# Start of a two-layer transformer kernel: the second x tile's statistics moved to ScalarE, the first rstd to GpSimd, and x tiles 2 and 3 loaded one Wq quarter later each

## Chip, cores and metric

The kernel runs on one core of one Trainium2 chip. The metric is the device time of one execution in microseconds. The profile's "span" is the part of an execution that the trace covers. It is somewhat shorter than the timed execution.

## The reference, cut to what matters

```
x = x + attention(layernorm(x))     # wqkv 1024 x 3072, sliding dilated window, wo
x = x + ffn(layernorm(x))           # 1024 -> 3584 -> 1024, gelu
# the same two lines once more (second layer, same weights)

def _layernorm(x, axis=-1, eps=1e-5):
    m = mean(x); v = var(x)
    return (x - m) / sqrt(v + eps)
```

The input x is 2048 x 1024 in bf16, which the kernel holds as 16 tiles of 128 rows. Nothing can be multiplied before the first tiles are loaded, normalised and transposed. The change is about that start alone.

## The kernel before

The first group of work is x tiles 0 to 3 and the weight Wq in four quarters of 512 KB, here called A to D. All are loaded by SP, in this order:

```
load_x(0, 0, 2)                        # x tiles 0 and 1
for k in range(0, KD, 2):
    load_wq_piece(wq_first[...], k)    # one quarter of Wq
    if k < 4:
        load_x(0, 2 + k // 2, 3 + k // 2)
# order: x0 x1 A x2 B x3 C D
```

The normalisation of the four tiles, in program order on VectorE (`vec`, DVE in the profile) and on ScalarE (`act`):

```
def stats(tt):
    ... two bn_stats and one bn_aggr on vec -> mvs[tt]
    act.activation(stds[tt][:], mvs[tt][:, 1:2], ACT.Sqrt, bias=eps_t[:])

def norm(tt, bounds=(0, D)):
    vec.reciprocal(rstd[:], stds[tt][:])
    ... vec.tensor_scalar: (x - mean) * rstd -> xn

stats(0); stats(1)
xn0 = norm(0); xn1 = norm(1, (0, 2 * P, D))
... 16 transposes of xn0 and xn1 on TensorE
stats(2); stats(3)
for tt in range(2, 4):
    first_late.append((norm(tt), ...))   # transposed later, among the matmuls
```

TensorE (PE) first runs 14 warm-up matmuls on zeros, then the transposes of tiles 0 and 1, then 36 half-width matmuls with quarters A to C, the transposes of tile 2, 16 more matmuls, the transposes of tile 3, and from there one unbroken run of 540 matmuls.

Of the kernel before, what the change touches and what calls it, by code (L numbers as in the profile page):

```python
# [8 lines left out]
ACT = mybir.ActivationFunctionType  # L9
ALU = mybir.AluOpType  # L10
AX = mybir.AxisListType
BF16 = mybir.dt.bfloat16
F32 = mybir.dt.float32
# [4 lines left out]
def kernel(  # L18
# [18 lines left out]
    P = 128  # L37
    _, S, D = A_x.shape
# [31 lines left out]
    lnp = ctx.enter_context(tc.tile_pool(name="lnp", bufs=2))  # L70
# [32 lines left out]
    vec, act, pool, sp = InOrder(nc.vector), InOrder(nc.scalar), InOrder(nc.gpsimd), InOrder(nc.sync)  # L103
# [15 lines left out]
    x = [xpool.tile([P, D], BF16, name=f"x{t}") for t in range(S // P)]  # L119

    def load_x(g, t0=0, t1=NTT):
        for tt in range(t0, t1):
            t = g * NTT + tt
            sp.dma_start(x[t][:], x_in[t * P:(t + 1) * P, :])
# [9 lines left out]
    def load_wq_piece(wt, k):  # L134
        sp.dma_start(wt[:, k % (KD // 2):k % (KD // 2) + 2, :], wqkv_v[:, k:k + 2, 0:D])
# [2 lines left out]
    wq_first = [wpool.tile([P, KD // 2, D], BF16, name="wt") for _ in range(2)]  # L138
    for k in range(0, KD, 2):
        load_wq_piece(wq_first[k // (KD // 2)], k)  # L140
        if k < 4:
            load_x(0, 2 + k // 2, 3 + k // 2)

    warm = bigp.tile([P, P], BF16, name="big")
    vec.memset(warm[:], 0.0)
    mhalf = const.tile([P, 1], F32, name="mhalf")
    pool.memset(mhalf[:], -0.5)
    eps_t = const.tile([P, 1], F32, name="eps_t")
# [59 lines left out]
    def transpose_on_pe(xn, out, parts):  # L208
        pst = psum.tile([P, KD, P], BF16, name="acc", bufs=8)
        for k in range(parts[0][0], parts[-1][1]):  # L210
            pe(nc.tensor.transpose(pst[:, k, :], xn[:, k * P:(k + 1) * P], ident[:]))  # L211
        for k0, k1, copy in parts:
            copy(out[:, k0:k1, :], pst[:, k0:k1, :])
# [10 lines left out]
    def ln_first():  # L224

        xa[0] = new_xnT()
        vec.on = act.on = True
        mvs = {}
        stds = {}

        def stats(tt):
            st6 = lnp.tile([P, 2, 6], F32, name="stats")
            for h in range(2):
                vec.bn_stats(st6[:, h, :], x[tt][:, h * HALF:(h + 1) * HALF])
            mvs[tt] = lnp.tile([P, 2], F32, name="mv")
            vec.bn_aggr(mvs[tt][:], st6[:])
            stds[tt] = lnp.tile([P, 1], F32, name="std")
            act.activation(stds[tt][:], mvs[tt][:, 1:2], ACT.Sqrt, bias=eps_t[:])

        def norm(tt, bounds=(0, D)):  # L240
            rstd = lnp.tile([P, 1], F32, name="rstd")
            vec.reciprocal(rstd[:], stds[tt][:])
            xn = lnp.tile([P, D], BF16, name="xn", bufs=3)
            for lo, hi in zip(bounds[:-1], bounds[1:]):
                vec.tensor_scalar(out=xn[:, lo:hi], in0=x[tt][:, lo:hi], scalar1=mvs[tt][:, 0:1], scalar2=rstd[:],
                                  op0=ALU.subtract, op1=ALU.mult)
            return xn

        stats(0)
        stats(1)  # L250
        xn0 = norm(0)
        xn1 = norm(1, (0, 2 * P, D))
        transpose_on_pe(xn0, xa[0][:, 0, :, :], [(0, 2, act.copy), (2, 8, act.copy)])
        transpose_on_pe(xn1, xa[0][:, 1, :, :], [(0, 2, vec.tensor_copy)])
        transpose_on_pe(xn1, xa[0][:, 1, :, :], [(2, 8, act.copy)])
        stats(2)
        stats(3)
        for tt in range(2, 4):
            first_late.append((norm(tt), xa[0][:, tt, :, :]))
        vec.on = act.on = False  # L260
        act.hold()

    def new_xnT(pool=None):
        return (pool or xnp).tile([P, NTT, KD, P], BF16, name="xnT")
# [350 lines left out]
    pool.on = True  # L615
    warm_up(14)
    ln_first()
    first = build_constants()
    with tc.tile_pool(name="early", bufs=1) as early:
# [62 lines left out]
```

## Time and profile before

| | before |
|---|---|
| time, median of 6 runs | 1230.29 us (1230.14 to 1230.75) |
| span of the profile | 1228.4 us |
| PE busy | 1221.6 us |
| 36 matmuls start, by the chain (8.26 by the timeline) | 8.40 us |
| weight loads of tile 2's transposes begin | 12.14 us |
| run of 540 matmuls starts | 14.89 us |

The prediction shows the chain and the timeline. Two views more are needed. First, PE's timeline, whose columns are start, length, engine, line, operation, output<-inputs, shape, count and, in brackets, the idle time before with its releaser:

```profile
0.99 6.02 PE L117 MATMUL acc<-big 128*128 128x512 bf16 x14 [0.99 <-DVE big L92]
7.05 1.35 PE L211 MATMUL acc<-ident,xn 128*128 128x128 bf16 x16
```

The warm-up matmuls were over at 7.01 us in this run, and the transposes came at once. Second, the list of DMA issues for two short stretches, one with x tile 3 (issued at 3.11 us) and one with quarter C (issued at 3.62 us). The last column is the time from issue to landing in us:

```profile
x<-in_A_x_dram SPq DMA_DIRECT2D x1, 256.0 KB, 6.8
wt<-in_A_wqkv_dram SPq DMA_DIRECT2D x1, 512.0 KB, 7.6
```

The tile landed at 9.9 us, the quarter at 11.2. The first x tile, with nothing in front of it, took 2.7 us. So a transfer issued at 3 us seems to spend most of its time behind the bytes in front of it.

### The profile page before, as it was taken

Reading aid. Unit: us, or ns where it says so; the run is one execution under the profiler, and the core shown is the slowest. Engines: PE = TensorE matmul, PEld = TensorE weight load, DVE = VectorE, ACT = ScalarE, POOL = GpSimd, SP = SyncE. Lnnn points to the kernel's source line nnn. Section 1 sums busy time; section 2 is a strip of 40 time slices with the busy share of each in tenths; the row PEclk is TensorE's granted clock in tenths of the full one; section 3 lists DMA queues with packets and bytes.
Section 4 is the critical chain, followed back from the end, with each engine's and each line's share of the span. In section 5 each row is a group of like instructions: output and inputs, shape, how many; then the busy total and the mean of one; then the engine's idle time right before and its main releaser. Section 6 shows DMA issues by size and latency. Waiting matters only on the chain.

```text
span 1228.4 us, 13955 instructions
## 1 busy us (share of the span) xinstructions
PE 1221.6 (99%) x5720; PEld 632.7 (52%) x5770; DVE 861.5 (70%) x912; ACT 315.6 (26%) x497; POOL 120.9 (10%) x219
## 2 busy tenths in 40 slices
PE   9999999999999999999999999999999999999998
PEld 7666544456444564446544465444654444444444
DVE  7999896998898999375993759937599797011001
ACT  5343253014310233202431024410244001300310
POOL 2330025010101101100001000000000002000000
PEclk9999999999999999999999999999999999999999
DMA  9965674766638645856557565576664558446441
GB/s 302 290 206 164 176 233 151 202 178 199 219 128 245 188 150 166 239 170 175 161 158 230 172 171 181 157 216 201 171 200 147 186 194 209 149 159 194 156 135 52
DMA packets 223647, 226.64 MB, mean 185 GB/s; under 512 B 71824, under 2 KB 190752, under 8 KB 221536
## 3 DMA queue, kind: packets, MB, share of 16 engines
q1 hardware_dynamic: 214704, 208.69, 56.3%
q0 software_dynamic: 8880, 17.07, 4.2%
q8 instruction: 45, 0.74, 0.2%
q14 instruction: 18, 0.15, 0.0%
HBM read 189.01 MB, written 4.19 MB: 157 GB/s over the span
## 4 chain that ended last, share of the span: by engine, by line
PE 99%; DVE 0%; issue 0%; DMA 0%
PE acc L117 99%; DMA x<-in_A_x_dram 0%; DVE stats L92 0%; PE acc L211 0%; DVE xn L92 0%; DVE x L92 0%; DVE mv L92 0%; DVE rstd L92 0%
## 5 line engine op out<-in xcount | busy, mean ns | idle before, releaser
L117 PE MATMUL acc<-xnT,wt 128*128 128x512 bf16 (+1 forms) x3392 | 720.3, 375 | 0.1
L117 PEld LDWEIGHTS <-wt 128*128 128x128 bf16 x3392 | 400.8, 120 | 317.4
L117 PE MATMUL acc<-wt,hT 128*128 128x512 bf16 (+1 forms) x1780 | 386.0, 376 | 2.1
L117 PEld LDWEIGHTS <-hT 128*128 128x128 bf16 x1820 | 178.1, 98 | 209.0
L92 DVE TENSOR_TENSOR big<-big 128x1024 bf16<-128x1024 bf16 (+2 forms) x184 | 244.8, 1359 | 2.2
L92 ACT ACTIVATE hT<-acc,b1T 128x512 bf16<-128x512 f32 x224 | 152.1, 687 | 325.9 <-PE acc L117 325.8
L92 DVE TENSOR_TENSOR big<-qT,kT 128x4096 bf16<-128x4096 bf16 x64 | 143.8, 2283 | 36.3 <-ACT kT L92 35.9
L92 DVE TENSOR_TENSOR big<-abc,vT 128x4096 bf16<-128x4096 bf16 x64 | 144.6, 2284 | 11.0 <-DMA abc<-a 7.1
L92 DVE TENSOR_TENSOR tmp<-acc,b2bc 128x512 f32<-128x512 f32 x56 | 38.6, 689 | 159.8 <-PE acc L117 156.7
L92 ACT CAST qT<-acc 128x512 bf16<-128x512 f32 (+1 forms) x72 | 38.0, 543 | 276.8 <-PE acc L117 274.6
L117 PE MATMUL acc<-wt,oT 128*128 128x512 bf16 x440 | 97.6, 379 | 0.4
L92 DVE BATCH_NORM_STATS2 stats<-x 128x6 f32<-128x512 bf16 x116 | 77.4, 681 | 6.0 <-DMA x<-in_A_x_dram 5.0
L117 PEld LDWEIGHTS <-oT 128*128 128x128 bf16 x448 | 43.8, 98 | 53.0 <-issue 0.3
L92 DVE TENSOR_TENSOR x<-acc,big 128x512 bf16<-128x512 f32 (+1 forms) x9 | 5.7, 632 | 90.0 <-PE acc L117 90.0
L92 POOL TENSOR_TENSOR rstd<-mv,eps_t 128x1 f32<-128x1 f32 x54 | 16.7, 308 | 524.2 <-DVE mv L92 524.2
L92 ACT CAST vT<-acc 128x512 bf16<-128x512 f32 x64 | 37.4, 585 | 101.9 <-PE acc L117 101.9
L92 ACT CAST kT<-acc 128x512 bf16<-128x512 f32 x64 | 37.3, 584 | 64.5 <-PE acc L117 64.5
L92 DVE TENSOR_TENSOR x<-acc,x 128x512 bf16<-128x512 f32 x64 | 42.9, 670 | 5.1 <-PE acc L117 4.7
L92 DVE TENSOR_SCALAR xn<-x,mv,rstd 128x1024 bf16<-128x1024 bf16 (+2 forms) x53 | 28.5, 540 | 20.1 <-POOL rstd L92 19.9
L92 DVE TENSOR_TENSOR x<-tmp,x 128x512 bf16<-128x512 f32 x56 | 38.6, 689 | 1.4
L92 POOL DMA_DIRECT2D big<-big x24 | 13.3, 563 | 212.5 <-DVE big L92 212.5
L92 ACT ACT_TABLE_LOAD x17 | 21.8, 1283 | 38.9 <-DVE e L92 30.5
(62 smaller groups left out, 285.4 us busy)
## 6 DMA issues: line engine op xcount, KB each, us to landing
wt<-in_B_w_dram SPq DMA_DIRECT2D x56, 1024.0 KB, 5.6
wt<-in_B_w_dram SPq DMA_DIRECT2D x64, 896.0 KB, 4.8
wt<-in_A_wqkv_dram SPq DMA_DIRECT2D x46, 1024.0 KB, 5.6
wt<-in_A_wo_dram SPq DMA_DIRECT2D x16, 1024.0 KB, 5.0
abc<-a POOLq DMA_DIRECT2D x32, 256.0 KB, 4.6
big<-big POOLq DMA_DIRECT2D x24, 256.0 KB, 3.8
x<-in_A_x_dram SPq DMA_DIRECT2D x16, 256.0 KB, 7.1
out_dram<-x SPq DMA_DIRECT2D x31, 128.0 KB, 1.8
```

What stands on the lines that cost most here:

```text
L92: inst = f(*args, **kwargs)
L117: return pe(nc.tensor.matmul(*args, **kwargs))
```

## The change

Its intent can be read from the diff. VectorE, which does all four tiles' statistics in turn, is to hand tile 1 to the idle ScalarE. Tile 0 is to be normalised without waiting for ScalarE. And the Wq quarters are to land sooner, so that an earlier PE finds them.

```
-        if k < 4:
-            load_x(0, 2 + k // 2, 3 + k // 2)
+        if 2 <= k < 6:
+            load_x(0, 1 + k // 2, 2 + k // 2)      # order: x0 x1 A B x2 C x3 D
 ...
-            act.activation(stds[tt][:], mvs[tt][:, 1:2], ACT.Sqrt, bias=eps_t[:])
+            if tt == 0:
+                rstds[tt] = lnp.tile([P, 1], F32, name="rstd")
+                pool.tensor_tensor(out=rstds[tt][:], in0=mvs[tt][:, 1:2], in1=eps_t[:], op=ALU.add)
+                pool.tensor_tensor(out=rstds[tt][:], in0=rstds[tt][:], in1=mhalf[:], op=ALU.pow)
+            else:
+                act.activation(stds[tt][:], mvs[tt][:, 1:2], ACT.Sqrt, bias=eps_t[:])
+
+        def stats_on_act(tt):
 ...
+            act.activation(junk[:], x[tt][:], ACT.Identity, scale=-1.0 / D, accum_out=less[:])
+            act.activation(junk[:], x[tt][:], ACT.Square, bias=less[:], accum_out=mvs[tt][:, 1:2])
+            act.activation(stds[tt][:], mvs[tt][:, 1:2], ACT.Sqrt, scale=1.0 / D, bias=eps_t[:])
 ...
         stats(0)
-        stats(1)
+        less = stats_on_act(1)
         xn0 = norm(0)
+        vec.tensor_scalar(out=mvs[1][:, 0:1], in0=less[:], scalar1=-1.0, scalar2=None, op0=ALU.mult)
         xn1 = norm(1, (0, 2 * P, D))
```

PE's own program is the same instruction for instruction.

More of the change, by code (lines that the diff above doesn't have):

```diff
@@ L228, in ln_first @@
         mvs = {}
-        stds = {}
+        stds, rstds = {}, {}
         def stats(tt):
@@ L237, in stats @@
             stds[tt] = lnp.tile([P, 1], F32, name="std")
-            act.activation(stds[tt][:], mvs[tt][:, 1:2], ACT.Sqrt, bias=eps_t[:])
+            if tt == 0:
[5 more added lines that the diff above has]
+        def stats_on_act(tt):
+            junk = lnp.tile([P, D], BF16, name="xn", bufs=3)
+            less = lnp.tile([P, 1], F32, name="less")
+            mvs[tt] = lnp.tile([P, 2], F32, name="mv")
+            act.activation(junk[:], x[tt][:], ACT.Identity, scale=-1.0 / D, accum_out=less[:])
+            act.activation(junk[:], x[tt][:], ACT.Square, bias=less[:], accum_out=mvs[tt][:, 1:2])
+            stds[tt] = lnp.tile([P, 1], F32, name="std")
+            act.activation(stds[tt][:], mvs[tt][:, 1:2], ACT.Sqrt, scale=1.0 / D, bias=eps_t[:])
+            return less
         def norm(tt, bounds=(0, D)):
-            rstd = lnp.tile([P, 1], F32, name="rstd")
-            vec.reciprocal(rstd[:], stds[tt][:])
+            rstd = rstds.get(tt)
+            if rstd is None:
+                rstd = lnp.tile([P, 1], F32, name="rstd")
+                vec.reciprocal(rstd[:], stds[tt][:])
             xn = lnp.tile([P, D], BF16, name="xn", bufs=3)
```

## The prediction

> **What bounds the kernel now.** I first read the page's busy shares and the chain that ended last, then cut that chain to the first 20 us, because the change touches nothing later. Over the whole run TensorE is the bound:
>
> ```profile
> PE 1221.6 (99%) x5720; PEld 632.7 (52%) x5770; DVE 861.5 (70%) x912; ACT 315.6 (26%) x497; POOL 120.9 (10%) x219
> PE 99%; DVE 0%; issue 0%; DMA 0%
> ```
>
> PE is busy 1221.6 us of a span of 1228.4 us. The table of busy time by stretches of 40 us has PE at 38.87 us in the first and at 39.79 us or more in every other one up to 1200 us. So after the start PE has no hole in which anything could be won or hidden, and a delay of PE in the first 15 us goes through to the end one for one. The whole question is when PE has worked off the three bursts of transposes in the start. The chain of waits in the first 20 us:
>
> ```profile
> 0.74 2.69 DMA x<-in_A_x_dram
> 3.46 1.30 DVE stats L92 x2
> ...
> 6.44 0.55 DVE xn L92
> ...
> 7.10 0.74 DVE xn L92 x2
> 7.84 0.05 issue
> 7.89 0.51 PE acc L211 x6
> 8.40 4.01 PE acc L117 x36
> 12.41 0.45 PE acc L211 x8
> 12.85 1.75 PE acc L117 x16
> ```
>
> Columns are start, length, what. First x tile, VectorE (DVE) statistics and normalisation of tiles 0 and 1, six transposes of tile 1, then 36 half-width matmuls, the eight transposes of tile 2 and 16 more matmuls, without a gap. The chain puts no wait before the transposes of tile 2, but the timeline shows how near one is:
>
> ```profile
> 8.03 1.28 DVE L92 BATCH_NORM_STATS2 stats<-x 128x6 f32<-128x512 bf16 x2
> 9.34 0.21 DVE L92 BATCH_NORM_AGGREGATE mv<-stats 128x2 f32<-128x12 f32 x1
> 9.93 1.29 DVE L92 BATCH_NORM_STATS2 stats<-x 128x6 f32<-128x512 bf16 x2 [0.38 <-DMA x<-in_A_x_dram]
> 11.25 0.21 DVE L92 BATCH_NORM_AGGREGATE mv<-stats 128x2 f32<-128x12 f32 x1
> 11.38 0.11 DVE L92 RECIPROCAL rstd<-std 128x1 f32<-128x1 f32 x1
> 11.53 0.55 DVE L92 TENSOR_SCALAR xn<-x,mv,rstd 128x1024 bf16<-128x1024 bf16 x1
> 12.14 0.54 PEld L211 LDWEIGHTS <-xn 128*128 128x128 bf16 x8
> ```
>
> VectorE runs in program order: statistics of tile 2, statistics of tile 3, only then the normalisation of tile 2. It sat idle 0.38 us until x tile 3 landed at 9.93 us. The normalised tile 2 was done at 12.08 and PE loaded its first weights from it at 12.14, just when its 36 matmuls were through. **Before is a tie**: landing of x tile 3 to the first transpose of tile 2 is 12.14 - 9.93 = 2.21 us of VectorE work that PE just meets. Whatever moves that landing later moves PE.
>
> **What the Trainium skill says.** (1) "DMA: Bandwidth & Descriptors", section "Queues, rings and completion order": on each DMA engine descriptors are consumed in ring order. All loads here are issued by SP, so the bytes queued ahead should set a load's landing. The trace agrees, as I work out below. (2) The same page, section "Anatomy of one DMA — SWDGE (gpsimd) path": most of the fixed cost of about 2 us is the completion after the last byte. That section is of the other issue path; the trace shows a lag of 1.3 to 1.5 us here. (3) "ScalarE: Activation LUTs", section "What ACT_TABLE_LOAD costs": an ACTIVATE takes 186 ns + 0.833 ns per element with immediates and about 280 ns + 0.833 ns with a pointer bias. At 1024 elements that is 1.04 and 1.13 us; the trace has 1.06 and 1.15 us for the same two passes at 27.33 and 28.51. (4) "TensorE: Matmul & The Clock Gate", Part 1: the clock is halved after an idle window of about 3.4 us. The stall that I expect is under 1 us, so I charge no cold clock; no stall of before can test that.
>
> **The transfers, step by step.** The bytes moved come from the table by stretches, last column GB/s:
>
> ```profile
> 2.00:4.00 2.00, 2.00 (x7) 0.65 (x5) 0.54 (x1) 0.23 (x2) 0.00 (x0) 1.00 0.90 285
> 4.00:6.00 2.00, 2.00 (x6) 0.72 (x5) 1.97 (x5) 0.29 (x1) 0.00 (x0) 1.00 0.96 250
> 6.00:8.00 2.00, 1.86 (x15) 0.83 (x14) 1.89 (x8) 0.59 (x3) 0.00 (x0) 1.00 1.05 379
> 8.00:10.00 2.00, 2.00 (x22) 1.99 (x21) 1.58 (x5) 1.77 (x4) 0.00 (x0) 1.00 1.03 390
> ```
>
> With 24 GB/s in the first 2 us, that sums to 0.62 MB at 4 us, 1.12 at 6, 1.88 at 8, 2.66 at 10. An x tile is 0.262 MB, a Wq quarter 0.524. Call the quarters A to D. Order before: x0 x1 A x2 B x3 C D, cumulated 0.26, 0.52, 1.05, 1.31, 1.84, 2.10, 2.62, 3.15 MB. On that curve B is through at 7.9, x3 at 8.6, C at 9.9 us. The list of DMA issues, asked for short stretches, gives landings: B issued 2.64 + 6.6 = 9.2 us; x3 3.11 + 6.8 = 9.9 us; and C 3.62 + 7.6 = 11.2 us. Each is 1.3 us behind the curve, so the ring-order model fits.
>
> Order after: x0 x1 A B x2 C x3 D, cumulated 0.26, 0.52, 1.05, 1.57, 1.84, 2.36, **2.62**, 3.15 MB. x3 now ends at the very place where C ended: landing about 11.25 us in place of 9.93, **1.32 us later**. x2 takes B's place: 9.2 in place of 7.95 us. A stays, B comes at about 8.6 (9.2 before), C at about 10.6 (11.2), D stays at about 12.8. DMA is saturated throughout, so reordering only moves lateness from the Wq quarters to x tiles 2 and 3.
>
> **The change part by part.**
> - Tile 0, rstd by GpSimd. It no longer waits for the statistics of tile 1 on VectorE. The group tile at 25.02 shows the price: its aggregate ended at 25.23, two GpSimd operations followed (0.38 and 0.55 us), and the normalisation started at 26.35, 1.12 us later. So from 4.99: start 6.11, end 6.66 us, in place of 6.44 and 6.99. That is 0.33 us earlier and worth **nothing**, since the 14 warm-up matmuls hold PE until 7.01.
> - Tile 1 on ScalarE. It removes two BATCH_NORM_STATS2 and an aggregate (1.4 us) from VectorE. It adds, from 27.33 to 29.76 in the trace of the same two passes, 2.43 us with both accumulator reads, and a square root of 0.29. No table load: the two passes at 27.33 ran with none. x1 landed at 1.19 + 3.1 = 4.3 us, so the square root ends near 4.3 + 0.05 + 2.43 + 0.29 = 7.07; with hand-offs the reciprocal starts at about 7.15 in place of 6.91. Tile 1 is then some **0.2 us later** and not earlier; PE's run of 36 matmuls starts at about 8.6 in place of 8.40 and is through at about 12.6.
> - Loads. Tile 3's statistics start at 11.25; plus the same 2.21 us, PE loads the first weights of tile 2 at **13.46** in place of 12.14. PE is there at 12.6 less its lead, so it stalls for about 0.8 us and the 0.2 us of tile 1 vanish inside the stall. Wq quarters were never waited for (no wait for DMA on PE or PEld in the list of waits), so their earlier landing wins nothing.
> - Behind it: tile 3 normalised at about 14.05, needed at 13.46 + 2.2 = 15.7; D landed at 12.8, needed after 14. No second stall. VectorE then starts group 1 about 0.75 us later (13.31 to 14.05), which the existing 1.50 us wait for an x tile at 21.85 takes up.
>
> Sum: +1.32 us, rounded up slightly for hand-offs to +1.35: 1230.35 + 1.35 = 1231.7 us.
>
> **The rivals.**
> - *The front is the bound.* If PE's start at 8.40 set the end and the x3 landing had slack, earlier normalisation could win up to about 0.4 us (transposes of both tiles back to back from 7.05: 16 x 0.057 = 0.91, so 7.96 in place of 8.40), giving 1229.9. For it: the chain does run through VectorE's statistics. Against: the 0.06 us tie at 12.14, the warm-up until 7.01 and x1's landing at 4.3.
> - *The wait is hidden.* If a later stage absorbed 1.3 us of PE, time would be 1230.4. Against: the 40 us table; I see no later hole of that size. If x tiles overtook the quarters in the rings, x3 would land near its old time and the result would be the same.
> - *It gets worse than a shift.* If PE cooled down in the stall, the next 3.4 us at half speed would add about 1.7 us, giving 1233.4. Against: PE idles under 1 us.
>
> **Range and chances.** The landing of x3 is good to some 0.4 us, the drift between runs is 0.5 us (1230.22 to 1230.75), and the rivals have perhaps one chance in six together. So 1230.9 to 1232.5 for 8 in 10. Two per cent is 25 us, far outside anything that the first 15 us can do: same 0.98, and 0.01 for each side, for a state of the chip that I don't see.
>
> **What would show it.** Right if: VectorE waits for x tile 3 until about 11.25; PE's weight loads wait about 0.8 us for the normalised tile 2 and resume near 13.5; the first burst of transposes still starts at 7.05; the later PE rows keep their counts and means, and the end is shifted by the delay at 15 us. Wrong if: x3 lands before 10.5; PE doesn't wait for tile 2; the table by stretches shows a second hole, or one closed, behind 20 us.

## The result, and the profile after

The changed kernel took **1232.36 us** (median of 6, 1231.28 to 1232.62), before 1230.29 us: 2.07 us more. The ratio of times is 1.0016, with an interval of 1.0003 to 1.0028. By the limit of 2% the two are the same. All that follows is about a fifth of a per cent, visible because the runs scatter by less than that.

The one profiled run was the fastest of the six, 1231.28 us. Its page and its chain, again cut to the start:

```profile
PE 1223.9 (100%) x5770; PEld 632.6 (51%) x5770; DVE 860.4 (70%) x909; ACT 317.9 (26%) x500; POOL 121.6 (10%) x221
```

```profile
3.63 7.22 DMA x<-in_A_x_dram
...
10.87 1.30 DVE stats L92 x2
...
12.46 0.56 DVE xn L92
...
13.06 0.62 PE acc L211 x8
13.68 1.76 PE acc L117 x16
```

PE's busy time is no larger in truth: the trace of before lacks 50 matmul records (5720 against 5770 weight loads), the one after lacks none. The chain is what changed. Before, it left the loads at x tile 0 and then followed VectorE and PE. Now it stays with one transfer, x tile 3, from its issue at 3.63 to its landing at 10.84 us, and goes on through that tile's statistics to tile 2's normalisation. The timeline shows both ends of it:

```profile
4.17 1.06 ACT L92 ACTIVATE xn<-x 128x1024 bf16<-128x1024 bf16 x1 [1.93 <-DMA x<-in_A_x_dram]
5.97 0.55 DVE L92 TENSOR_SCALAR xn<-x,mv,rstd 128x1024 bf16<-128x1024 bf16 x1 [0.94 <-POOL rstd L92]
6.58 0.62 PE L211 MATMUL acc<-ident,xn 128*128 128x128 bf16 x8
6.95 0.16 DVE L92 RECIPROCAL rstd<-std 128x1 f32<-128x1 f32 x1 [0.37 <-ACT std L92]
7.94 0.34 PEld L211 LDWEIGHTS <-xn 128*128 128x128 bf16 x6 [0.28 <-DVE xn L92]
8.84 1.29 DVE L92 BATCH_NORM_STATS2 stats<-x 128x6 f32<-128x512 bf16 x2 [0.68 <-DMA x<-in_A_x_dram]
10.87 1.29 DVE L92 BATCH_NORM_STATS2 stats<-x 128x6 f32<-128x512 bf16 x2 [0.49 <-DMA x<-in_A_x_dram]
13.06 0.45 PEld L211 LDWEIGHTS <-xn 128*128 128x128 bf16 x8 [0.86 <-DVE xn L92]
```

Tile 0 was normalised at 5.97 us and PE transposed it at 6.58. Then PE had to wait for tile 1, whose reciprocal started at 6.95 us where it had started at 6.91 before, and its last transposes began at 7.94 (7.88 before). The front has won nothing. VectorE then waited for x tile 2 and again for x tile 3, and PE's weight loads waited 0.86 us for tile 2 (PE itself 0.63) and got it at 13.06 us, not at 12.14. The run of 540 matmuls starts at 15.72 us, 0.83 us later than before, and the span is 0.8 us longer (1229.15 against 1228.36 us, unrounded).

That leaves two questions: why five runs of six were a further 1.1 to 1.3 us slower than this profile, and what happened outside the span. For the second, the list of runs gives the time and the span of every run:

| kernel | time less span |
|---|---|
| before, 23 runs in three sessions | 1.73 to 1.82 us |
| the changed kernel, 6 runs | 2.12 to 2.18 us |

So about 0.36 us of the loss lies where the trace doesn't look.

### The profile page after: what moved, and what is told of

Its sections match the earlier page's. It is cut to its first block, busy times and chain, and to the rows that moved or that the text cites. A ratio compares the mean times of both kernels' runs of the same rounds, so it can differ in the third digit from the quotient of the medians.

```text
span 1229.1 us, 14008 instructions
## 1 busy us (share of the span) xinstructions
PE 1223.9 (100%) x5770; PEld 632.6 (51%) x5770; DVE 860.4 (70%) x909; ACT 317.9 (26%) x500; POOL 121.6 (10%) x221
## 4 chain that ended last, share of the span: by engine, by line
PE 99%; DMA 1%; SPq 0%; DVE 0%; issue 0%
PE acc L117 99%; DMA x<-in_A_x_dram 1%; SPq L92 0%; DVE stats L92 0%; PE acc L211 0%; DVE xn L92 0%; DVE x L92 0%; DVE mv L92 0%; DVE rstd L92 0%
```

## The experiments

There were three sessions on three chips, each with its own runs of before (medians 1230.23, 1230.11 and 1230.13 us). Every kernel gave a correct result. "Span" is the median of the runs' spans.

| run | edit | time | before | span | before's span | time less span |
|---|---|---|---|---|---|---|
| e1_again | the change, one run | 1231.63 | 1230.23 | 1229.5 | 1228.5 | 2.13 |
| e2_old_loads | the new statistics alone | 1231.01 | 1230.23 | 1228.85 | 1228.5 | 2.13 to 2.20 |
| e3_loads_alone | the new load order alone | 1231.48 | 1230.23 | 1229.65 | 1228.5 | 1.75 to 1.85 |
| e4_norm2_first | the change, tile 2 normalised first | 1231.43 | 1230.23 | 1229.25 | 1228.5 | 2.16 to 2.20 |
| e5_pow_alone | GpSimd power alone | 1230.82 | 1230.11 | 1228.7 | 1228.3 | 2.11 to 2.20 |
| e6_act_alone | ScalarE passes alone | 1231.53 | 1230.11 | 1229.4 | 1228.3 | 2.12 to 2.15 |
| e7_x2_late | x tile 2 alone later | 1231.34 | 1230.11 | 1229.55 | 1228.3 | 1.75 to 1.82 |
| e8_x3_late | x tile 3 alone later | 1231.98 | 1230.11 | 1230.2 | 1228.3 | 1.74 to 1.80 |
| e9_two_memsets | two spare GpSimd memsets | 1230.30 | 1230.13 | 1228.55 | 1228.4 | 1.73 to 1.83 |
| e10_before_norm2 | before, tile 2 normalised first | 1230.62 | 1230.13 | 1228.8 | 1228.4 | 1.75 to 1.83 |
| e11_again | the change, four runs | 1232.29 | 1230.13 | 1230.15 | 1228.4 | 2.13 to 2.19 |
| e12_x3_late_norm2 | e8 with tile 2 normalised first | 1230.06 | 1230.13 | 1228.3 | 1228.4 | 1.74 to 1.82 |

How much of this is clear of noise? Only the change itself has an interval of the ratio that leaves out 1, in its first measurement and in e11 (1.0002 to 1.0029); a single run (e1) has none. The runs of e3, e4, e6, e7 and e8 (four each) nevertheless all lie above every run of before in their session. Those of e2, e5, e9, e10 and e12 overlap with before's, so differences of up to 0.8 us there are weak evidence. The time less span is much sharper: its two groups never overlap.

### First session: the two halves apart

**e1_again** is the changed kernel unaltered.

> The changed kernel once more, unaltered, for a second profile. Its six runs were 1231.28 (the profiled one) and five of 1232.33 to 1232.62, so its one trace shows the exception. Theory A (x tile 3 lands later in most runs): a run near 1232.4 shows the statistics of x tile 3 starting about 1.1 us later than the 10.87 us of the first profile. Theory B (PE's clock drops after the stall): a run near 1232.4 shows x tile 3 at about 10.9 us again, and PE slower for some microseconds after 13 us. If this run is near 1231.3 it decides nothing.

At 1231.63 us it fell between the two levels. The statistics of x tile 3 started at 11.23 us and not at 10.87, 0.36 later, and the span is 0.33 us longer (1229.48 against 1229.15 us, unrounded). This speaks for theory A and decides little. It also shows another thing that varies: x tile 1 landed at 5.0 us in this run (1.19 + 3.8), not at 4.2, so tile 1's reciprocal came only at 7.84 us. The end didn't feel it, but only just: the 36 matmuls were over at 13.33 us and tile 2 came at 13.43.

**e2_old_loads** undoes the load order.

```
-        if 2 <= k < 6:
-            load_x(0, 1 + k // 2, 2 + k // 2)
+        if k < 4:
+            load_x(0, 2 + k // 2, 3 + k // 2)
```

> The changed statistics with the loads in the order of before. My theory (the landing of x tile 3 is all of the loss): VectorE starts the statistics of x tile 3 near 9.9 us, PE meets the normalised tile 2 without a wait near 12.2 us, time 1230.3 us, within 0.3 of before. Rival (the new statistics cost time themselves, tile 1 being ready later): 1230.7 us or more. Rival (the new statistics win and the loads hide it): 1230.0 or less.

The chain of its profile no longer holds a wait for x tile 3:

```profile
8.28 4.06 PE acc L117 x36
12.34 0.45 PE acc L211 x8
12.78 1.76 PE acc L117 x16
```

PE meets tile 2 without a gap, as in before, at 12.34 us where before had 12.41. So the mechanism was as expected. The time was not: 1231.01, or 0.78 us over before, the size that the first rival had named. Of that, 0.36 us lies outside the span (medians 2.17 and 1.81) and 0.35 us in the spans of the other runs, which were 1228.7 to 1229.0. Those runs left no trace, and what held them up is not shown.

**e3_loads_alone** makes the same edit the other way round, the new load order in the kernel before.

> Before with the new load order alone. My theory: x tile 3 lands 1 us or more later, PE waits 0.8 us or more for the normalised tile 2, time 1231.3 to 1232.5 us, the same as the whole change. Rival (the statistics carry the loss): 1230.3 us.

The time was 1231.48 us, 1.25 more than before, and nearly all of it is span (+1.15). PE's timeline shows the wait:

```profile
8.11 4.33 PE L117 MATMUL acc<-xnT,wt 128*128 128x256 bf16 x36
14.20 0.62 PE L211 MATMUL acc<-ident,xn 128*128 128x128 bf16 x8 [1.76 <-DVE xn L92]
```

The loads cost 1.25 us and the statistics 0.78, together 2.03, against 2.07 for the whole in its first measurement. For the 0.36 us outside the span that is as it should be, as only one half brings it. For the rest the agreement is partly luck: a late front would be hidden behind the late tile 2 and should not add, and the spans of the changed kernel alone range over 1.4 us. The single run of the whole taken beside these two, e1, was 1.40 us over before.

**e4_norm2_first** keeps the whole change and breaks the dependence of tile 2 on x tile 3.

```
-        stats(2)
-        stats(3)
         for tt in range(2, 4):
+            stats(tt)
             first_late.append((norm(tt), xa[0][:, tt, :, :]))
```

> The whole change, but VectorE normalises tile 2 before it starts the statistics of tile 3, so that tile 2 no longer hangs on the landing of x tile 3. My theory: tile 2 is normalised near 11.4 us, PE, which comes there at 12.2, doesn't wait, and tile 3 at 13.8 is ready before PE needs it at 14.4; time 1230.3 us, within 0.3 of before, with the new load order kept. Rival (late Wq quarters, a cooled PE or anything else in the new order costs the time): 1231 us or more.

This missed: 1231.43 us. In the profiled run x tile 2 landed at 10.02 us, so tile 2 was late by itself, and behind it stood a second wait that I hadn't counted. PE's timeline, and then lines of the chain:

```profile
12.74 0.62 PE L211 MATMUL acc<-ident,xn 128*128 128x128 bf16 x8 [0.22 <-DVE xn L92]
...
15.47 0.61 PE L211 MATMUL acc<-ident,xn 128*128 128x128 bf16 x8 [0.35 <-ACT xnT L92]
```

```profile
2.64 7.38 DMA x<-in_A_x_dram
...
12.68 1.21 DVE stats L92 x2
...
14.22 0.30 ACT std L92
14.52 0.91 ACT xnT L92
```

On ScalarE the copy of the transposed tile 2 stands behind the square root of tile 3. That square root waited for tile 3's statistics, which VectorE began as soon as it had normalised tile 2; x tile 3 itself had landed at 12.0 us (3.63 + 8.4). PE's transposes of tile 3 waited for the copy, to 15.47 us, but tile 3 was itself normalised only at 15.30. So both waits go back to x tile 2, the other tile that the new order moves. In this one profile nothing waits for x tile 3. And 0.36 us of this kernel's 1.20 lie outside the span, which the expectation had not allowed for.

### Second session: each part alone

**e5_pow_alone** and **e6_act_alone** have the old load order. In the first, tile 1's statistics stay on VectorE and only the first rstd goes to GpSimd; in the second, tile 1 goes to ScalarE and the first rstd keeps its square root.

> Before with one part alone: the first rstd by GpSimd power; statistics of tile 1 on VectorE and loads as before. All kernels with the new statistics so far took 2.12 to 2.20 us outside the profile's span, all others 1.73 to 1.85. Theory P (the GpSimd power costs the 0.38 us outside the span): time less span 2.16 us, time 1230.6. Theory S (the ScalarE passes cost it): time less span 1.79 us, time 1230.2 to 1230.3. Inside the span no change is expected, as the warm-up matmuls hold PE.

> Before with one part alone: tile 1's statistics in two ScalarE passes; first rstd by square root on ScalarE and loads as before. In program order the first square root (about 5.0 us, after VectorE's statistics of tile 0) now stands before the passes, which start near 5.3 in place of 4.2 us. Expected: tile 1 normalised about 1.1 us later than in the whole change, PE's run of 36 matmuls starts near 9.3 us and not near 8.2, and no wait for tile 2 behind it; time 1231.2 to 1231.7. Time less span: 1.79 us by theory P, 2.16 us by theory S.

Theories P and S both fell. Each part alone has the 0.36 us outside the span: 2.11 to 2.20 us with the power, 2.12 to 2.15 with the passes. Inside the span, e5 was 0.4 us longer, though its profile has PE's 36 matmuls starting at 8.07 us by the timeline (8.26 in before), early rather than late. What PE waited for was a Wq quarter:

```profile
11.79 1.09 PE L117 MATMUL acc<-xnT,wt 128*128 128x256 bf16 x8 [0.28 <-DMA wt<-in_A_wqkv_dram]
```

Before has some runs of that length too (spans up to 1229.0 beside e5, untraced), so whether the power has a part in this is not shown. e6 did as expected: the first square root at 5.13 us holds the passes back, the last transposes of tile 1 start at 9.10 us in the chain, and the time is 1231.53 us.

```profile
5.13 0.30 ACT std L92
5.43 1.05 ACT xn L92 x2
...
9.10 0.51 PE acc L211 x6
```

This shows what the GpSimd power is for. It gains no time by itself, but without it ScalarE's passes start later: by the timeline at 5.34 us, against 4.17 in the changed kernel and 3.99 in e2.

**e7_x2_late** and **e8_x3_late** each move one x tile of the kernel before.

```
e7:  -  if k < 4:            load_x(0, 2 + k // 2, 3 + k // 2)
     +  if k == 2:           load_x(0, 2, 4)                      # x0 x1 A B x2 x3 C D
e8:  -  if k < 4:            load_x(0, 2 + k // 2, 3 + k // 2)
     +  if k in (0, 4):      load_x(0, 2 + k // 4, 3 + k // 4)    # x0 x1 A x2 B C x3 D
```

> Before with x tile 2 alone moved behind the second Wq quarter (x0 x1 A B x2 x3 C D). x tile 3 has the same bytes ahead of it as before (2.10 MB in all). My theory (only the landing of x tile 3 counts): it lands near 9.9 us again, time 1230.2 to 1230.5 us. Rival (x tile 2's landing counts, or two quarters in a row slow the start of the transfers down): 1231 us or more.

> Before with x tile 3 alone moved behind the third Wq quarter (x0 x1 A x2 B C x3 D). My theory: it carries the whole loss of the new load order, x tile 3 landing near 11.2 us and PE waiting for the normalised tile 2: 1231.2 to 1231.8 us, as the new load order alone (1231.48). Rival (the two in a row at the start, or x tile 2): 1230.3 us.

e8 behaved as expected in kind, at 1231.98 us, 1.87 over before and 0.2 above the range expected. VectorE started x tile 3's statistics at 12.03 us, where about 11.2 was expected:

```profile
12.03 1.29 DVE L92 BATCH_NORM_STATS2 stats<-x 128x6 f32<-128x512 bf16 x2 [1.85 <-DMA x<-in_A_x_dram]
```

e7 did not: 1231.34 us, 1.23 over before, so the theory that only x tile 3 counts fell. VectorE's timeline says why:

```profile
9.95 1.29 DVE L92 BATCH_NORM_STATS2 stats<-x 128x6 f32<-128x512 bf16 x2 [1.73 <-DMA x<-in_A_x_dram]
11.40 1.23 DVE L92 BATCH_NORM_STATS2 stats<-x 128x6 f32<-128x512 bf16 x2
12.94 0.55 DVE L92 TENSOR_SCALAR xn<-x,mv,rstd 128x1024 bf16<-128x1024 bf16 x1
```

With x tile 2 at 9.93 us, both tiles' statistics, 1.45 us from one start to the next, stand in a row in front of the normalisation. Tile 2 follows the later of two times: the landing of x tile 3, and that of x tile 2 plus 1.45 us. In the changed kernel x tile 3 is the later one by the 0.49 us that VectorE waited for it.

### Third session: the spread, the rest outside the span, and a better order

**e9_two_memsets** asks whether added instructions as such bring the 0.36 us.

```
     pool.memset(eps_t[:], EPS)
+    spare = const.tile([P, 1], F32, name="spare")
+    for _ in range(2):
+        pool.memset(spare[:], 0.0)
```

> Before plus two GpSimd memsets of a spare 128x1 tile in the preamble, with no other edit. The GpSimd power alone and the ScalarE passes alone each took 2.11 to 2.20 us outside the span, before 1.73 to 1.82. Theory L (any change of the instruction streams can shift this part): 2.15 us, time 1230.5 to 1230.8. Theory N (it belongs to the new operations or their waits): 1.79 us, time 1230.1 to 1230.3.

These two don't: 1.73 to 1.83 us, as before. What brings it stays open. All five kernels with either new statistics part have it, in all 27 runs; no run of another kernel has it, and the traces can't show it.

**e10_before_norm2** makes the edit of e4 in the kernel before, for a version that beats both.

> Before, loads unchanged, with tile 2 normalised before the statistics of tile 3. My theory: the tie on the landing of x tile 3 is gone, tile 2 is normalised near 10.7 us, and what remains are PE's start at 8.4 and the landing of the third Wq quarter. Spans of 1228.2 to 1228.5 in all runs where before has 1228.2 to 1229.0: time 1230.0 to 1230.2, less than before by 0.1 to 0.2. Rival (late runs of before come from the third Wq quarter): no change, 1230.2 with the same spread.

The rival was right: 1230.62 against 1230.13 us, ratio 1.0 with an interval of 0.9988 to 1.0013. In the profiled run, the slowest of the five, PE waited 0.29 us for the third Wq quarter, which landed at 11.9 us. The kernel before has two near ties, tile 2 and the third quarter, and freeing one gained nothing that these runs show.

**e11_again** is the changed kernel once more.

> The changed kernel unaltered once more, timed and profiled. From the parts: 1.15 us in the span from the loads, 0.3 in the span and 0.37 outside it from the statistics, so 1231.8 to 1232.3 us. Theory A (spread comes from the transfers): in this profile the span follows the start of the statistics of x tile 3 as span = start + 1218.25 us, as in the two profiles so far (10.87 and 1229.1, 11.23 and 1229.5). Theory B (a cooled PE): a span above that.

The median was 1232.29 us, 2.16 over before: 0.36 outside the span (medians 2.16 and 1.80), 1.75 in it. The profiled run shows the start of x tile 3's statistics and the wait of PE behind it, from the views of VectorE and of PE's weight loads:

```profile
11.77 1.29 DVE L92 BATCH_NORM_STATS2 stats<-x 128x6 f32<-128x512 bf16 x2 [0.50 <-DMA x<-in_A_x_dram]
13.96 0.45 PEld L211 LDWEIGHTS <-xn 128*128 128x128 bf16 x8 [1.64 <-DVE xn L92]
```

Theory A put the span at 11.77 + 1218.25 = 1230.0 us; it was 1229.9. Theory B finds nothing: the 16 matmuls after a wait of 1.64 us took 1.75 us in the chain, as in before. So the spread of the changed kernel is the spread of a landing. By the same sum, the spans of 1230.2 to 1230.5 us of the five slower runs answer to a start at about 11.95 to 12.25 us; that is an estimate, as those runs left no trace.

**e12_x3_late_norm2** joins e8's load order with tile 2 normalised first.

> Before with x tile 3 alone moved behind the third Wq quarter, and tile 2 normalised before the statistics of tile 3. My theory: tile 2 depends on x tile 2 alone, which lands as before, and x tile 3, landing 1.3 us later, is normalised near 13.9 us, before PE needs it at 14.4: time 1230.0 to 1230.4 us in place of the 1231.98 of the same load order with the old order on VectorE. Rival (x tile 3's lateness can't be hidden, since its square root stands ahead of the copy of tile 2 on ScalarE): 1230.8 us or more.

It took 1230.06 us beside before's 1230.13, where e8 had lost 1.87 us with the same loads. x tile 3 was late again, but tile 2 no longer asked for it:

```profile
10.28 0.55 DVE L92 TENSOR_SCALAR xn<-x,mv,rstd 128x1024 bf16<-128x1024 bf16 x1
11.51 1.29 DVE L92 BATCH_NORM_STATS2 stats<-x 128x6 f32<-128x512 bf16 x2 [0.68 <-DMA x<-in_A_x_dram]
13.66 0.55 DVE L92 TENSOR_SCALAR xn<-x,mv,rstd 128x1024 bf16<-128x1024 bf16 x1
```

The normalisation of tile 2 starts at 10.28 us. That of tile 3 starts at 13.66 and ends at 14.21, and PE loads its first weights from it at 14.25, a near tie again. In the changed kernel a start of x tile 3's statistics at 11.51 us would go with a span of 1229.8 us, by the sum of e11; here it was 1228.1. This is the cleanest proof of the mechanism. It is no version that beats before: the ratio is 1.0 with an interval of 0.9986 to 1.0013.

## Why the prediction was right, point by point

The time lay in the range, near its top. Mechanism and sign were right; two terms of the sum were mis-sized, one of them by leaving it out. That the total still fell in the range, 0.14 us under its top, was partly luck: the width was meant for the landing and the drift, and it also took up a cost that nobody had counted.

- **PE bounds, a delay goes through one for one: right.** The span less the start of the run of 540 matmuls is 1213.5 us before, 1213.4 in the first profile after and 1213.3 in e11.
- **Ring order sets the landings: right as a difference.** From the landing of quarter A to that of x tile 3 it took 2.7 us before (9.9 - 7.25), and 4.0 and 4.1 us in the two profiles after (10.84 - 6.86, 11.74 - 7.66). That is 1.3 to 1.4 us more; the prediction had 1.32. The old order varies too (3.1 us in e2, 9.83 - 6.76), so single pairs of profiles give 0.9 to 1.4. Over all profiles of these two orders it was 2.6 to 2.8 us in five of the old and 3.1 in e2, and 4.0 to 4.1 in all five of the new.
- **"landing about 11.25 us": mis-sized.** This took the byte curve of one profile as the curve of every run. Quarter A, third in every order, landed anywhere from 6.76 (e2) to 7.96 us (e8) over the profiles of all kernels, with no relation to the order that I can see: 6.76 to 7.96 with an x tile next, 6.86 to 7.96 with quarter B next. The changed kernel hides none of such lateness: its x tile 3 landed at 10.84, 11.21 and 11.74 us in three profiles, and the span followed. Whether before hides part of it is not shown.
- **"worth nothing, since the 14 warm-up matmuls hold PE until 7.01": right in effect, wrong in reason.** After, the warm-up was over at 6.44 us and tile 0's transposes came at 6.58, so the sign "first burst of transposes still starts at 7.05" failed. Over the profiles the warm-up ended between 5.47 (e12) and 7.08 us (e3). "TensorE: Matmul & The Clock Gate", Part 1, leads one to expect such a spread: it describes a clock gate that opens by a free-running window. The trace agrees: PE's weight loads in the warm-up of e12 come 0.43 us apart until 3.53 us and about 0.22 apart from there, in before 0.43 apart to the end. The gain was void because tile 1 came no sooner. The GpSimd path was mis-sized too, at 0.94 us for the 1.12 assumed.
- **Tile 1 "0.2 us later": not shown.** Its reciprocal started at 6.95 us against 6.91, and at 7.84 in e1, where x tile 1 landed late. A dependence on that landing has taken the place of one on VectorE's queue, and both are hidden behind tile 2.
- **"Wq quarters were never waited for": right of that one trace only.** PE waited for the third quarter for 0.29 us in e10, 0.28 in e5 and 0.38 in e7. So an earlier landing of the quarters may be worth a few tenths in late runs of before, as long as tile 2 is not later still.
- **2.21 us from the statistics of tile 3 to PE: right.** It was 2.19 us in the first profile after (10.87 to 13.06) and in e11 (11.77 to 13.96).
- **A stall of "about 0.8 us", no cooled clock: right.** The weight loads waited 0.86 us in the first profile; 1.64 us in e11 left the clock as it was.
- **The sum, "+1.35": short by 0.7 to 0.8 us.** In e11's session it was 1.75 us in the span and 0.36 outside it. The first misses by the landings above; the second was no term of the sum at all.

## What to carry to other kernels

When a load is moved behind another one, write down the bytes ahead of each transfer in both orders: the tile that gains bytes lands later by those bytes over the measured rate, and what its consumer does in program order decides whether that is seen. Look for ties before shuffling loads, since in a tuned start several waits end within a few tenths of a microsecond and moving one resource only changes which of them ends last. A change of dependence on one engine's order, as in e12, can pay for the whole transfer.

## What the Trainium skill lacked or had wrong

- "DMA: Bandwidth & Descriptors": the section "Anatomy of one DMA — SWDGE (gpsimd) path" gives a constant fixed part of about 2 us, for the other issue path. In the loads issued by SP here, landings lay 1.3 to 1.5 us behind the byte curve. In the first 8 us the landing of quarter A, third in every order, varied by 1.2 us between the profiles of all kernels (6.76 to 7.96 us), and by 0.8 us between the three of the changed kernel. That section has no figure for such a spread.
- "ScalarE: Activation LUTs", section "What ACT_TABLE_LOAD costs": the times for one ACTIVATE fit (1.06 us after, 1.04 by its formula), but an accumulator output adds an instruction of its own, 0.19 us, which the page doesn't list. From the start of one pass to the next it was 1.18 us (4.17 to 5.35).
- "GPSIMD Engine Reference": I found no time for a power on a 128 x 1 tile. Here it took 0.56 us, and from the end of the aggregate to the normalisation, with the addition, 0.94 us (5.03 to 5.97).
- "Runtime: NRT & Kernel Launch", section "The ~15µs preamble/postamble breakdown", names a gap of about 6.2 us between profile and execution time, the same for every kernel, by which the profile is the longer. The gap here is another one: the timed execution is longer than the traced span, by 1.73 to 1.85 us in all kernels with the old statistics and by 2.11 to 2.20 us in all with a new part of them. I found no page on that difference, and its cause is open.
